# Block 2's accumulators loaded during the projections, and eight of phi_q's last sixteen stores put behind attention's first loads

## The chip, the cores and the metric

The kernel runs on one core of a Trainium2 chip. The metric is the device time of one execution in microseconds. The core has five engines that matter here: TensorE (PE) for matmuls, VectorE (DVE), ScalarE (ACT) and GpSimd (POOL) for elementwise work, and SyncE (SP), whose queue issues nearly all DMA transfers of this kernel. Every engine takes its own instructions strictly in order; an instruction that waits for another engine holds up everything behind it on its own engine.

## The reference

One layer on x of 2048 tokens by 640 features: x is normalised, and the sum of x, a linear attention and an MLP is returned.

```python
def _A_ref(x, wqkv, w_phi, wo):                     # 32 heads of 20
    q, k, v = ...(x @ wqkv)
    pq, pk = q @ w_phi, k @ w_phi                   # per head
    phi_q = concatenate([softmax(pq), softmax(-pq)], -1)
    phi_k = concatenate([softmax(pk), softmax(-pk)], -1)
    kv = einsum("bhsf,bhsd->bhfd", phi_k, v)
    z  = einsum("bhsf->bhf", phi_k)
    o  = (phi_q @ kv) / (phi_q @ z + 1e-6)
    return o @ wo

def _B_ref(x, w1, b1, w2, b2):                      # 640 -> 1728 -> 640
    return gelu(layernorm(x) @ w1 + b1) @ w2 + b2

xn = layernorm(x)
return x + _A_ref(xn, ...) + _B_ref(xn, ...)
```

All values are float32. The kernel splits every float32 operand of a matmul into a high and a low part (`hi`, `lo`) and multiplies high by high, high by low and low by high, three matmuls for each product (`mm3`, lines 69 to 72).

## The kernel before, in words

The 2048 tokens are four blocks of 512, held transposed (features on the 128 partitions). The program has these stages, and the order of work on PE is written out by hand for all of them:

1. The MLP of blocks 0 and 1, with the preparation of the projection weights and of blocks 2 and 3 beside it. At its end the accumulators of both blocks, `acc0` and `acc1`, are stored to DRAM (line 879, the arrays `a0` and `a1`), since their place in SBUF is wanted for something else.
2. The projections (loop at line 1021): for each of 16 token tiles t, four groups i of matmuls (line 910) make q, k and v, already multiplied by the feature map's weights. `k_tile` and `q_tile` make the softmax features with ACT, DVE and POOL; `kv_tile` adds phi_k^T V into five PSUM banks. `q_tile` turns phi_q (DVE, line 1007) into places that lie in the old tiles `acc0` and `acc1` and in one more tile, `et`. Four tiles make one block b; `store_phi(b, n)` (line 1009) writes quarter n of block b to the DRAM array `e`, with four DMAs for each quarter, so sixteen for a block. Block 3's quarters 0 and 1 lie in `acc1`, quarter 2 in `et`, quarter 3 in `acc0`.
3. The first weight pair of the MLP of blocks 2 and 3 (`passes(0, 2)` and `passes(0, 3)`, lines 1106 and 1336). Line 1111 and 1112 load x of these blocks as the accumulators `acc2` and `acc3`, and line 1114 loads combinations of both blocks, `tf`. All of these lie on the right side of SBUF, where the projection weights had been, so their loads wait for the last projection matmul. The coroutine `finish_kv` runs beside the second pass: it issues the sixteen stores of block 3's phi_q, and then turns the kv sums into the attention's weights `kvs` in three groups of small matmuls (lines 1148, 1148 and 1156). Each group has a PSUM bank: the first 3, the second 4, the third 3 again. DVE reads a group's bank with L1138 and L1140 and then helps to split it (ACT L61, DVE L64).
4. Weight pairs 1 to 5 for blocks 2 and 3 together (`Mlp.cross`, lines 420 to 515): seven products of sums of weights and sums of blocks. They go into three banks a, b and c, some of which ACT has to copy out (`copy`, line 455) before the next product may go in. Its weights come from DRAM into the raw tiles r1 and r2 (first layer at line 362, second layer at line 360), are added up into the tile `s` by POOL (`Mlp.sums`, line 393), and are split: ACT makes a high part (line 398), POOL a low part (line 399), but for the sums `s`, where DVE makes it (line 399 too). Attention runs beside these products: `Attention.load` reads phi_q back from `e` (lines 1174 and 1176), `first` splits it (ACT L1205, POOL L1206), and `second` multiplies it by `kvs` on PE (lines 1212 and 1213).
5. The last pair, the output projection and the stores.

Three things set the order around the change. Between lines 877 and 1355 the instructions of DVE, ACT and POOL are put into order by the framework's scheduler, by its own estimate of times; PE's order is the written one throughout, and from line 1355 on that of the other three as well. SP's order is always the scheduler's. Work "beside" PE is attached to ticks: `mlp.tick()` is called after each group of matmuls, and `mlp.after(n, step)` runs a step n ticks later. And `tc.issue_after(x)` keeps what is in it behind the instruction x.

```python
            copy(z22, "b")
            product("a", "s2", "t2")
            copy(z12, "a")
            next(before)
            later[1]()
            next(before)
            product("a", "s3", "t3")
```

These lines (482 to 488) are the part of `cross` where bank a is copied out by ACT and filled again; `later[0]`, called a few lines earlier, is the first half of the split of the pair's second-layer weights.

Of the kernel before, what the change touches and what calls it, by code (L numbers as in the profile page):

```python
# [8 lines left out]
F32 = mybir.dt.float32  # L9
F32R = mybir.dt.float32r  # L10
# [5 lines left out]
P = 128  # L16
S, D, F, H, DH = 2048, 640, 1728, 32, 20
KC = D // P
# [28 lines left out]
def f(ap):  # L47
    return ap.bitcast(F32)
# [3 lines left out]
def tile_kernel(ctx: ExitStack, tc: tile.TileContext, x, xT, wkT, wqT, wv, wphi, wo, w1, b1, w2, b2,  # L52
                ident, mmask, emask, vsel, out):
    nc = tc.nc
# [33 lines left out]
    e_dram = [tc.dram_tile([2 * D, 512], F32, name=f"e{b}") for b in range(NB)]  # L88
# [9 lines left out]
    acc = [None] * NB  # L98
# [18 lines left out]
    rp = ys.enter_context(tc.tile_pool(name="raw", bufs=1))  # L117
# [101 lines left out]
    class Mlp:  # L219
# [166 lines left out]
        def sums(self, g, apart=0):  # L386

            raw = [r.rearrange("p (c f) -> p c f", f=P) for r in self.raw[g, False]]
            (a11, a12), (a21, a22) = ((r[:, 0:4:2, :], r[:, 1:4:2, :]) for r in raw)
            s = rp.tile([P, 3, 2, P], F32, name="s")  # L390
            for i, (out, x0, x1, op) in enumerate(((s[:, 0], a21, a22, ALU.add), (a21, a11, a21, ALU.subtract),
                                                   (s[:, 1], s[:, 0], a11, ALU.subtract), (s[:, 2], a12, s[:, 1], ALU.subtract))):
                self.after(i * apart, lambda out=out, x0=x0, x1=x1, op=op: nc.gpsimd.tensor_tensor(out, x0, x1, op=op))
            self.raw[g, "s"] = s
# [122 lines left out]
    def load_acc(b):  # L517
        nc.sync.dma_start(acc[b], xT[:, b * 512:(b + 1) * 512].rearrange("(c p) t -> p c t", p=P))
# [4 lines left out]
    mlp = Mlp((0, 1, 2, 3), ((0, 2), (1, 3)))  # L523
# [358 lines left out]
    kvp = [banks.tile([P, 512], F32, name=f"bank{i}") for i in (3, 4, 5, 6, 7)]  # L882
    ptile = Banks(0, 1, 2)

    es = ExitStack()
    et = es.enter_context(tc.tile_pool(name="eT", bufs=1, reuse_waits="tile"))
    a = ExitStack()
# [11 lines left out]
    def proj(t, i):  # L899

        yh, yl = y[t // 4]
        c = slice((t % 4) * P, (t % 4) * P + P)
        wh, wl = [w[:, :, slice(*CB[i])] for w in wkv_] if i < 3 else wv_
        ps = ptile()[:, :wh.shape[2]]
        ops = [(lh, rh, kc) for kc in range(KC) for lh, rh in ((yh, wh), (yh, wl), (yl, wh))]
        if i == 3:

            ops.sort(key=lambda op: op[1] is wh)
        for n, (lh, rh, kc) in enumerate(ops):
            nc.tensor.matmul(ps, lh[:, kc, c], rh[:, kc], start=n == 0, stop=n == 3 * KC - 1)  # L910
        return ps
# [97 lines left out]
    def store_phi(b, n):  # L1009

        ed = e_dram[b][320 * n:320 * n + 320, :].rearrange("(j r) (q n) -> q r j n", r=32, q=4)
        for q in range(4):
            nc.sync.dma_start(ed[q], ets[b][n][32 * q:32 * q + 32])  # L1013
# [7 lines left out]
    for t, i in [(t, i) for t in range(14) for i in range(4)] + TAIL:  # L1021
        if (t, i) in ((4, 0), (8, 0)):
            b = t // 4 + 1
            y[b] = [yp.tile([P, KC, 512], F32R, name=f"y{p}{b % 2}") for p in range(2)]
            for p in range(2):
                nc.sync.dma_start(f(y[b][p]), y_dram[b - 2][p])
        ps = proj(t, i)
        pq = 1 + t % 3
        if t and t % 4 == 0:
            store_phi(t // 4 - 1, i)  # L1030
        if i == 0:
            evac = evacuate(ps, 0, 0)
        elif i == 1:
            evac = evacuate(ps[:, :KQ - 512], 0, 512 // H)
            fts[t] = k_tile(t)
            evacuate(ps[:, KQ - 512:], pq, 0)
        elif i == 2:
            evacuate(ps[:, C3 - C2:], pq, B1F)
            v_parts(t, ps, VF)
            q_tile(t)  # L1040
        else:
            evac = v_parts(t, ps, 0)

        tk = {(15, 1): 13, (15, 3): 14}[t, i] if (t, i) in ((15, 1), (15, 3)) else t - 2 if 1 < t < 15 and i == 0 else None
        if tk is not None:
            kv_tile(tk, fts.pop(tk), vbuf[tk % 2])
        if i == 0 and t in (1, 2, 3, 6, 7):

            kc = (1, 2, 3, 6, 7).index(t)
            lo = rp.tile([P, D], F32, name="r1")  # L1050
            hi = rp.tile([P, D], F32R, name="r2")
            nc.sync.dma_start(lo, wo[kc * P:(kc + 1) * P, :])
            with tc.issue_after(evac):
                split(hi, lo.bitcast(F32R), lo, eng=nc.gpsimd)
            for w, wd in zip((f(hi), lo), wo_dram):
                nc.sync.dma_start(wd[:, kc, :], w)
        if (t, i) == (11, 0):
            mlp = Mlp((0, 3, 2, 1), ((1, 2), (0, 3)))
            mlp.ph = ptile
            mlp.fetch_pair(0, False)  # L1060
        if (t, i) == (12, 3):
            with tc.issue_after(evac):
                w1t, parts = mlp.take_pair(0, False, 0)
                for part in parts:
                    part()
            mlp.fetch_pair(0, True)
        if (t, i) == (15, 3):
            w2t, late = mlp.take_pair(0, True, 3)
            late.pop(0)()
# [11 lines left out]

    accp = ctx.enter_context(tc.tile_pool(name="acc23", bufs=1, side="right", reuse_waits="tile"))
    bp = ctx.enter_context(tc.tile_pool(name="bconst", bufs=1, side="right", reuse_waits="tile"))
    for b in range(2, 4):
        acc[b] = accp.tile([P, KC, 512], F32, name=f"acc{b}")
    kvs = bp.tile([P, 11, P], F32R, name="kvs")
    tfp = ctx.enter_context(tc.tile_pool(name="turned", bufs=1, side="right", reuse_waits="tile"))
    tf = [tfp.tile([P, 3, 2, 512], F32R, name=f"tf{q}") for q in range(2)]  # L1090
# [17 lines left out]
        next(before)  # L1108
    for _ in mlp.beside:
        pass  # L1110
    load_acc(2)
    load_acc(3)
    for q in range(2):
        nc.sync.dma_start(f(tf[q]), t_dram[q][:, 1:4])
# [10 lines left out]
    def finish_kv(pxt):  # L1125


        with tc.issue_after(subs["q", 15].ins):
            nc.gpsimd.memset(f(kvs), 0.0)
        for n in range(14):  # L1130
            if n > 9:
                store_phi(3, n - 10)
            yield

        def done(tp, dens, mask, hi, lo):

            r, n, w = tp.shape
            nc.vector.tensor_scalar_add(dens, dens, DEN_EPS)  # L1138
            km = sp.tile([G6, 5, VR], F32, name="km", bufs=1)[:r, :n, :w]
            nc.vector.tensor_tensor(km, tp, mask.unsqueeze(1).to_broadcast(list(km.shape)), op=ALU.mult)  # L1140
            split(hi, lo, km)

        for o in range(2):
            tp = pxt()
            for c in range(5):
                nc.tensor.matmul(tp[:G6, c * VR:(c + 1) * VR], t1[:, c, o], sel, start=True, stop=True)
            kg = kvs[:G6, 0:10].rearrange("p (c o) v -> p o c v", o=2)[:, o]
            done(tp[:G6, :5 * VR].rearrange("p (c v) -> p c v", c=5),  # L1150
                 tp[:G3, :5 * VR].rearrange("p (c a b) -> p c a b", c=5, a=2)[:, :, :, 30:32],
                 mm_t, kg[:, :, 64 * o:64 * o + VR], kg[:, :, 64 - 64 * o:64 - 64 * o + VR])
            yield
        tp = pxt()
        for c, d in ((0, slice(0, 30)), (52, slice(30, 40)), (30, slice(40, 42))):
            nc.tensor.matmul(tp[:80, d], kxs, sel[:XM, c:c + d.stop - d.start], start=True, stop=True)
        tp = tp[:80, :42].unsqueeze(1)
        done(tp, tp[0:40, :, 40:42], em_t, kvs[:80, 10:11, 0:42], kvs[:80, 10:11, 64:106])

    class Attention:  # L1160
# [8 lines left out]
        def load(self, g):  # L1169

            e = self.es[g] = ep.tile([P, 512], F32, name="e", bufs=6)
            r = g * G6
            n = min(P, 2 * D - r)
            nc.sync.dma_start(e[:n], e_dram[self.b][r:r + n, :])
            if n < P:
                nc.sync.dma_start(e[n:], e_dram[self.b][0:P - n, :])

# [152 lines left out]
    at, copies = {}, Banks(3, 4)  # L1330
# [26 lines left out]
    def gathered(g):  # L1357
# [6 lines left out]

        return w2t, [parts[0], second, lambda: g < 5 and mlp.sums(g + 1, 1)]

    for g in range(1, 6):
        w2t, later = gathered(g)
        hid, more = mlp.cross(g, (2, 3), before, later)
        if g < 5:  # L1370
            parts = mlp.splits(g + 1)
        else:
            w1t, parts = mlp.take_pair(6, False, 1)
        for m, _ in enumerate(mlp.second(g, 2, w2t, hid[0])):
            next(more, None)
            if m < len(parts):
                parts[m]()
            if m == 3:
                mlp.fetch_pair(g + 1, True)
        before = mlp.second(g, 3, w2t, hid[1])  # L1380
# [7 lines left out]
    sums, turned, accs = [], {}, {}  # L1388
# [38 lines left out]

    def place_sums():
        sums.append(wp.tile([P, 4, D], F32R, name="w3").rearrange("p i d -> p (i d)"))
        sums.extend([bp.tile([P, 11, P], F32R, name="kvs").rearrange("p i d -> p (i d)"), rp.tile([P, 3, 2, P], F32R, name="s").rearrange("p i k n -> p (i k n)")])  # L1430

    def lo_part(c, k):
        n = (c + 4 * k) * 256
# [233 lines left out]
```

## Time and profile before

| | |
|---|---|
| time, median of 3 runs | 703.58 us (702.67 to 705.65) |
| profiled execution, its own time | 703.39 us |
| its span, first to last instruction | 701.6 us |
| PE busy | 694.9 us (99%) |
| DVE, ACT, POOL busy | 527.6, 365.1, 455.9 us |
| DMA | 107.62 MB, mean 153 GB/s |
| granted TensorE clock, mean | 1.000 |

The page lists busy time, the span in 40 slices, the DMA queues, the chain that ended last, and the costliest groups. In the lists of waits a line names the engine and line that waited and what it waited for. In the timelines each line has the start in us from the span's start, the length in us, engine, source line, operation, output<-input and the count; a bracket at the end says how long the engine was idle before it and what ended that. The span is shorter than the execution's own time by what lies around it.

### The profile page before, as it was taken

Reading aid. Unit: us, or ns where it says so; the run is one execution under the profiler, and the core shown is the slowest. Engines: PE = TensorE matmul, PEld = TensorE weight load, DVE = VectorE, ACT = ScalarE, POOL = GpSimd, SP = SyncE. Lnnn points to the kernel's source line nnn. Section 1 sums busy time; section 2 is a strip of 40 time slices with the busy share of each in tenths; the row PEclk is TensorE's granted clock in tenths of the full one; section 3 lists DMA queues with packets and bytes.
Section 4 is the critical chain, followed back from the end, with each engine's and each line's share of the span. In section 5 each row is a group of like instructions: output and inputs, shape, how many; then the busy total and the mean of one; then the engine's idle time right before and its main releaser. Section 6 shows DMA issues by size and latency. Waiting matters only on the chain.

```text
span 701.6 us, 9805 instructions
## 1 busy us (share of the span) xinstructions
PE 694.9 (99%) x3331; PEld 584.8 (83%) x3331; DVE 527.6 (75%) x859; ACT 365.1 (52%) x617; POOL 455.9 (65%) x388
## 2 busy tenths in 40 slices
PE   9999999999999999999999999999999999999998
PEld 7888888888788888888888888878888888888886
DVE  7868654977744788788888888838688687789783
ACT  6534643344334544554544536557676667659350
POOL 4711314576245997798787969558689997577930
PEclk9999999999999999999999999999999999999999
DMA  9824633485621227425500707974345648881222
GB/s 330 266 100 130 195 105 99 159 276 171 214 105 76 81 89 224 96 80 201 133 1 1 192 0 261 276 226 118 120 146 160 187 145 293 282 283 60 76 76 105
DMA packets 67464, 107.62 MB, mean 153 GB/s; under 512 B 7622, under 2 KB 31974, under 8 KB 65790
## 3 DMA queue, kind: packets, MB, share of 16 engines
q1 hardware_dynamic: 67110, 106.98, 47.6%
q8 instruction: 26, 0.43, 0.2%
q14 instruction: 24, 0.20, 0.1%
q10 hardware_dynamic: 304, 0.01, 0.0%
HBM read 72.42 MB, written 34.55 MB: 152 GB/s over the span
## 4 chain that ended last, share of the span: by engine, by line
PE 75%; DVE 10%; POOL 6%; issue 4%; DMA 3%; ACT 2%; SPq 1%; POOLq 0%; DVEq 0%; ACTq 0%
PE bank L910 17%; PE bank L70 16%; PE bank L72 16%; PE bank L71 16%; POOL m L945 2%; POOL m L956 2%; PE bank L648 2%; PE bank L1212 1%; PE bank L1213 1%; PE bank L980 1%; DVE w L64 1%; SPq L1013 1%; DVE mx L934 1%; DVE acc L1007 1%; PE bank L554 1%
## 5 line engine op out<-in xcount | busy, mean ns | idle before, releaser
L910 PE MATMUL bank<-wkh,y 128*128 128x512 f32 (+1 forms) x480 | 139.5, 364 | 0.0
L70 PE MATMUL bank<-m,w 128*128 128x512 f32 x288 | 113.1, 393 | 0.5 <-DVE acc L337 0.3
L64 POOL TENSOR_TENSOR w<-r,w 128x640 fp32r<-128x640 f32 x32 | 52.6, 1658 | 93.1 <-ACT w L61 62.2
L71 PE MATMUL bank<-m,w 128*128 128x512 f32 x288 | 112.1, 389 | 0.0
L72 PE MATMUL bank<-m,w 128*128 128x512 f32 x266 | 103.6, 389 | 0.0
L70 PE MATMUL bank<-y,w 128*128 128x512 f32 (+1 forms) x256 | 99.6, 389 | 0.0
L71 PE MATMUL bank<-y,w 128*128 128x512 f32 (+1 forms) x256 | 98.9, 386 | 0.0
L910 PEld LDWEIGHTS bank<-wkh,y 128*128 128x128 f32 x480 | 87.5, 188 | 13.3
L72 PE MATMUL bank<-y,w 128*128 128x512 f32 (+1 forms) x246 | 94.9, 386 | 0.0
L910 PE MATMUL bank<-wkl,y 128*128 128x512 f32 (+1 forms) x240 | 87.4, 364 | 0.0
L946 ACT ACTIVATE m<-m,rs_all 128x1280 f32<-128x1280 f32 x32 | 43.7, 1365 | 43.5 <-POOL m L945 43.4
L70 PEld LDWEIGHTS bank<-m,w 128*128 128x128 f32 x288 | 54.1, 188 | 12.5 <-DVE acc L337 0.7
L71 PEld LDWEIGHTS bank<-m,w 128*128 128x128 f32 x288 | 54.1, 188 | 10.9
L72 PEld LDWEIGHTS bank<-m,w 128*128 128x128 f32 x266 | 49.9, 188 | 10.5
L948 DVE TENSOR_REDUCE sm<-m 128x64 f32<-128x1280 f32 x32 | 47.4, 1482 | 14.9 <-ACT m L946 14.8
L910 PE MATMUL bank<-w,y 128*128 128x512 f32 x240 | 57.4, 391 | 0.0
L945 POOL TENSOR_TENSOR m<-m,mx 128x640 f32<-128x640 f32 (+2 forms) x48 | 44.4, 939 | 19.2 <-DVE mx L934 19.2
L70 PEld LDWEIGHTS bank<-y,w 128*128 128x128 f32 x256 | 48.1, 188 | 10.4 <-ACT bank L1280 0.3
L71 PEld LDWEIGHTS bank<-y,w 128*128 128x128 f32 x256 | 48.1, 188 | 9.4
L337 DVE TENSOR_TENSOR acc<-bank,acc 128x512 f32<-128x512 f32 x70 | 46.9, 683 | 11.8 <-PE bank L72 6.6
L72 PEld LDWEIGHTS bank<-y,w 128*128 128x128 f32 x246 | 46.2, 188 | 9.4
L910 PEld LDWEIGHTS bank<-w,y 128*128 128x128 f32 x240 | 44.4, 188 | 8.5
(236 smaller groups left out, 1542.1 us busy)
## 6 DMA issues: line engine op xcount, KB each, us to landing
r<-in_w SPq DMA_DIRECT2D x52, 320.0 KB
e<-e SPq DMA_DIRECT2D x40, 256.0 KB
e<-acc SPq DMA_DIRECT2D x52, 160.0 KB
t<-t SPq DMA_DIRECT2D x8, 512.0 KB
acc<-in_xT SPq DMA_DIRECT2D x3, 1280.0 KB
tf<-t SPq DMA_DIRECT2D x2, 1536.0 KB
xb<-in_x SPq DMA_DIRECT2D x8, 320.0 KB
t<-in_x SPq DMA_DIRECT2D x8, 320.0 KB
```

What stands on the lines that cost most here:

```text
L64: eng.tensor_tensor(lo, src, f(hi), op=ALU.subtract)
L70: nc.tensor.matmul(ps, lh, rh, start=first, stop=False, **kw)
L71: nc.tensor.matmul(ps, lh, rl, start=False, stop=False, **kw)
L72: nc.tensor.matmul(ps, ll, rh, start=False, stop=last, **kw)
L337: nc.vector.tensor_tensor(acc[b][:, m, :], pw, acc[b][:, m, :], op=ALU.add)
L554: nc.tensor.matmul(pz[j], wc[j][wi][:, kc, :], y[0][yi][:, kc, cols], start=(wi, yi, kc) == (0, 0, 0), stop=last[j] == op)
L648: nc.tensor.matmul(ps[:, u * nh * DF:(u + 1) * nh * DF], raw[:nh * DH, u * P:(u + 1) * P], wpt[:nh * DH, g, :nh, 1:], start=True, stop=True)
L910: nc.tensor.matmul(ps, lh[:, kc, c], rh[:, kc], start=n == 0, stop=n == 3 * KC - 1)
L945: subs[n, t] = nc.gpsimd.tensor_tensor(ep[:, s], a, b, op=ALU.subtract)
L946: exps[n, t] = nc.scalar.activation(e, e, AF.Exp, scale=rs_all[:, t:t + 1])
L948: nc.vector.tensor_reduce(sm, e.rearrange("p s (h f) -> p (s h) f", f=DH), axis=AX, op=ALU.add)
L956: nc.gpsimd.tensor_tensor(e3, e3, w.unsqueeze(2).to_broadcast([P, 2 * H, DH]), op=ALU.mult)
```

## The change

Four things are edited. The accumulators of block 2 get a place of their own, allocated ahead of the projections' tiles where the preparation of stage 1 had been, and their load is written inside the projections' loop, at t = 9. Only block 3's stay on the right side. The tile `s` moves from the pool of the raw weights (`rp`) to that of `kvs` (`bp`), which makes up part of the room. In `finish_kv` only quarters 2 and 3 of block 3 are stored; quarters 0 and 1 are stored 12 and 16 ticks into the loop over pairs 1 to 5, behind the last load that attention's block 0 has issued by then.

```diff
@@ -387,7 +387,7 @@
             (a11, a12), (a21, a22) = ((r[:, 0:4:2, :], r[:, 1:4:2, :]) for r in raw)
-            s = rp.tile([P, 3, 2, P], F32, name="s")
+            s = bp.tile([P, 3, 2, P], F32, name="s")
@@ -882,6 +882,7 @@
+    acc[2] = ctx.enter_context(tc.tile_pool(name="acc2", bufs=1)).tile([P, KC, 512], F32, name="acc2")
     es = ExitStack()
@@ -1054,6 +1055,8 @@
+        if (t, i) == (9, 0):
+            load_acc(2)
         if (t, i) == (11, 0):
@@ -1081,10 +1084,9 @@
-    accp = ctx.enter_context(tc.tile_pool(name="acc23", bufs=1, side="right", reuse_waits="tile"))
+    accp = ctx.enter_context(tc.tile_pool(name="acc3", bufs=1, side="right", reuse_waits="tile"))
     bp = ctx.enter_context(tc.tile_pool(name="bconst", bufs=1, side="right", reuse_waits="tile"))
-    for b in range(2, 4):
-        acc[b] = accp.tile([P, KC, 512], F32, name=f"acc{b}")
+    acc[3] = accp.tile([P, KC, 512], F32, name="acc3")
@@ -1108,7 +1110,6 @@
-    load_acc(2)
     load_acc(3)
@@ -1128,7 +1129,7 @@
         for n in range(14):
-            if n > 9:
+            if n > 11:
                 store_phi(3, n - 10)
             yield
@@ -1171,7 +1172,7 @@
-            nc.sync.dma_start(e[:n], e_dram[self.b][r:r + n, :])
+            self.last = nc.sync.dma_start(e[:n], e_dram[self.b][r:r + n, :]).ins
@@ -1364,6 +1365,12 @@
+    def late_store(n):
+        with tc.issue_after(at[0].last):
+            store_phi(3, n)
+
+    for n in range(2):
+        mlp.after(12 + 4 * n, lambda n=n: late_store(n))
     for g in range(1, 6):
@@ -1427,7 +1434,7 @@
-        sums.extend([bp.tile([P, 11, P], F32R, name="kvs").rearrange("p i d -> p (i d)"), rp.tile([P, 3, 2, P], F32R, name="s").rearrange("p i k n -> p (i k n)")])
+        sums.extend([bp.tile([P, 11, P], F32R, name="kvs").rearrange("p i d -> p (i d)"), bp.tile([P, 3, 2, P], F32R, name="s").rearrange("p i k n -> p (i k n)")])
```

No instruction on PE changes its place, and POOL's order stays as well. On three engines the order moves. Lines after 393 are one to three higher in the changed kernel.

SP, from the end of the first pair to the start of `cross`, before (the first of the sixteen stores stands a little ahead, between loads of y; `e_73` is the DRAM array of block 3's phi_q, `e_70` that of block 0; `acc_2046` is `acc1`, `acc_2045` is `acc0`; `r_4360` and `r_4361` are the raw second-layer weights of pair 1, `r_4460` and `r_4461` the first-layer weights of pair 2):

```order
L1013 DMA e_73<-acc_2046 32x10x128 x7
L1013 DMA e_73<-et 32x10x128 x4
L1013 DMA e_73<-acc_2045 32x10x128 x4
L360 DMA r_4360<-in_w 128x640
L360 DMA r_4361<-in_w 128x640
L1174 DMA e<-e_70 80x512
L1176 DMA e<-e_70 48x512
L1174 DMA e<-e_70 128x512 x5
L362 DMA r_4460<-in_w 128x640
L362 DMA r_4461<-in_w 128x640
```

The same place in the changed kernel (`acc_2050` is `acc1` there, `acc_2049` is `acc0`):

```order
L1014 DMA e_73<-et 32x10x128 x4
L1014 DMA e_73<-acc_2049 32x10x128 x4
L360 DMA r_4355<-in_w 128x640
L360 DMA r_4356<-in_w 128x640
L1175 DMA e<-e_70 80x512
L1177 DMA e<-e_70 48x512
L1175 DMA e<-e_70 128x512 x4
L1014 DMA e_73<-acc_2050 32x10x128 x4
L1175 DMA e<-e_70 128x512
L1014 DMA e_73<-acc_2050 32x10x128 x4
L362 DMA r_4459<-in_w 128x640
L362 DMA r_4460<-in_w 128x640
```

Eight stores have moved from ahead of the weights' loads L360 to behind attention's loads, and now stand ahead of the loads L362. Block 2's accumulator load (L518) has moved too: it now stands far ahead, between the two stores of `a0` and `a1` at line 879.

ACT, from the evacuation of block 3's hidden layer (L292, L61) to the kv matmuls, before (`r_4112`, `r_4113` are the raw first-layer weights of pair 1, `s` their sums, `w_4352` and `w_4353` the split weights):

```order
L292 ACTIVATE m_4219<-bank_4221,b1t 128x512
L61 ACTIVATE m_4220<-m_4219 128x512
L292 ACTIVATE m_4219<-bank_4242,b1t 128x512
L61 ACTIVATE m_4241<-m_4219 128x512
L398 ACTIVATE w_4352<-r_4112 128x640
L398 ACTIVATE w_4353<-r_4113 128x640
L61 ACTIVATE kvs<-km 120x5x64
L398 ACTIVATE w_4353<-s 128x768
```

The same place in the changed kernel:

```order
L292 ACTIVATE m_4222<-bank_4224,b1t 128x512
L398 ACTIVATE w_4347<-r_4117 128x640
L61 ACTIVATE m_4223<-m_4222 128x512
L292 ACTIVATE m_4222<-bank_4245,b1t 128x512
L61 ACTIVATE m_4244<-m_4222 128x512
L398 ACTIVATE w_4348<-r_4118 128x640
L398 ACTIVATE w_4348<-s 128x768
L61 ACTIVATE kvs<-km 120x5x64 x2
```

The first split of pair 1's weights has moved up by three places, and the split of the sums stands ahead of both splits of `kvs`.

DVE at the kv matmuls, before (`bank_4301` is the bank of the first group, `bank_4315` of the second, `bank_4331` of the third; L335 adds a finished bank to block 2's accumulators):

```order
L335 SCALAR_TENSOR_TENSOR acc_4123<-bank_4281,b2t,acc_4123 128x512
L1138 TENSOR_SCALAR bank_4301<-bank_4301 60x10x2
L1140 TENSOR_TENSOR km<-bank_4301,mm_t 120x320
L335 SCALAR_TENSOR_TENSOR acc_4123<-bank_4297,b2t,acc_4123 128x512
L1138 TENSOR_SCALAR bank_4315<-bank_4315 60x10x2
L64 TENSOR_TENSOR kvs<-km,kvs 120x5x64
L1140 TENSOR_TENSOR km<-bank_4315,mm_t 120x320
L1138 TENSOR_SCALAR bank_4331<-bank_4331 40x2
L399 TENSOR_TENSOR w_4353<-s,w_4353 128x768
```

The same place in the changed kernel:

```order
L335 SCALAR_TENSOR_TENSOR acc_2026<-bank_4276,b2t,acc_2026 128x512
L399 TENSOR_TENSOR w_4348<-s,w_4348 128x768
L1139 TENSOR_SCALAR bank_4296<-bank_4296 60x10x2
L1141 TENSOR_TENSOR km<-bank_4296,mm_t 120x320
L335 SCALAR_TENSOR_TENSOR acc_2026<-bank_4292,b2t,acc_2026 128x512
L64 TENSOR_TENSOR kvs<-km,kvs 120x5x64
L1139 TENSOR_SCALAR bank_4310<-bank_4310 60x10x2
L1141 TENSOR_TENSOR km<-bank_4310,mm_t 120x320
```

The low part of the sums, L399, has moved from behind all three groups to ahead of the first group's evacuation.

## Rows read from the trace of the kernel before

**Rows 1.** The page's part 1: busy us (share of the span) xinstructions.

```profile
PE 694.9 (99%) x3331; PEld 584.8 (83%) x3331; DVE 527.6 (75%) x859; ACT 365.1 (52%) x617; POOL 455.9 (65%) x388
```

**Rows 2.** The waits of PE: engine, line, waited for: us, times, longest us.

```profile
PE bank L582 <- POOL m L580: 1.3, 1, 1.3
PE bank L70 <- ACT m L455: 1.2, 1, 1.2
PE bank L70 <- DVE acc L337: 0.3, 1, 0.3
```

**Rows 3.** PE in order of time, 463.8 to 466.1: start, length, instruction [idle before].

```profile
463.83 0.39 PE L71 MATMUL bank<-m,w 128*128 128x512 f32 x1
464.06 0.39 PE L72 MATMUL bank<-m,w 128*128 128x512 f32 x1
465.67 0.50 PE L70 MATMUL bank<-tf,w 128*128 128x512 f32 x1 [1.22 <-ACT m L455]
```

**Rows 4.** ACT in order of time, 459 to 466.

```profile
459.24 0.63 ACT L464 ACTIVATE m<-m 128x512 fp32r<-128x512 f32 x1
462.28 0.74 ACT L398 ACTIVATE w<-r 128x640 fp32r<-128x640 f32 x1 [2.41 <-DMA r<-in_w]
462.93 0.58 ACT L455 ACTIVATE m<-bank 128x512 f32<-128x512 f32 x1
464.50 0.63 ACT L1205 ACTIVATE m<-e 128x512 fp32r<-128x512 f32 x1 [1.00 <-DMA e<-e]
465.04 0.58 ACT L455 ACTIVATE m<-bank 128x512 f32<-128x512 f32 x1
```

**Rows 5.** SP's queue in order of time, 446 to 469: issues of DMAs.

```profile
446.66 4.91 SPq L1013 DMA_DIRECT2D e<-acc  x7
...
454.58 2.93 SPq L1013 DMA_DIRECT2D e<-acc  x4
457.63 1.31 SPq L360 DMA_DIRECT2D r<-in_w  x2
...
460.01 2.59 SPq L1174 DMA_DIRECT2D e<-e  x5
464.69 3.69 SPq L362 DMA_DIRECT2D r<-in_w  x2
```

**Rows 6.** POOL in order of time, 444 to 475.

```profile
444.32 0.74 POOL L393 TENSOR_TENSOR s<-r 128x256 f32<-128x256 f32 x1 [1.67 <-DMA r<-in_w]
447.87 1.81 POOL L399 TENSOR_TENSOR w<-r,w 128x640 fp32r<-128x640 f32 x1 [2.81 <-ACT w L398]
...
451.83 1.83 POOL L399 TENSOR_TENSOR w<-r,w 128x640 fp32r<-128x640 f32 x1
...
474.29 0.75 POOL L393 TENSOR_TENSOR s<-r 128x256 f32<-128x256 f32 x1
```

**Rows 7.** Stretch by stretch: busy us (x) of PE, PEld, DVE, ACT, POOL; PEclk, DMA share, GB/s.

```profile
200.00:220.00 20.00, 20.00 (x94) 16.85 (x93) 9.08 (x18) 5.86 (x11) 10.58 (x11) 1.00 0.32 132
```

**Rows 8.** ACT in order of time, 444 to 453.

```profile
444.30 0.69 ACT L292 ACTIVATE m<-bank,b1t 128x512 f32<-128x512 f32 x1 [2.34 <-DVE m L64]
445.08 0.63 ACT L61 ACTIVATE m<-m 128x512 fp32r<-128x512 f32 x1
...
447.06 0.73 ACT L398 ACTIVATE w<-r 128x640 fp32r<-128x640 f32 x1
...
451.91 0.85 ACT L398 ACTIVATE w<-s 128x768 fp32r<-128x768 f32 x1 [0.41 <-POOL s L393]
```

**Rows 9.** DVE in order of time, 449 to 455.

```profile
449.26 0.18 DVE L1138 TENSOR_SCALAR bank<-bank 60x20 f32<-60x20 f32 x1 [0.33 <-PE bank L1148]
449.48 0.49 DVE L1140 TENSOR_TENSOR km<-bank,mm_t 120x320 f32<-120x320 f32 x1
...
452.80 1.68 DVE L399 TENSOR_TENSOR w<-s,w 128x768 fp32r<-128x768 f32 x1
```

**Rows 10.** PE in order of time, 449 to 452: the third kv group.

```profile
451.57 0.53 PE L1156 MATMUL bank<-sel,kxs 123*80 123x30 f32 x6
```

## The prediction

> **What bounds the kernel now.** The engine part of the page comes first: PE is busy for 694.9 of the 701.6 us of the span [rows 1]. The other four engines have room, so only what makes PE stand still, or what puts work onto it, can move the time. The change adds and removes no matmul; what it can win is therefore in the waits of PE [rows 2]. Two of them are longer than half a microsecond: 1.3 us right at the start of the program, before the warming matmuls, which nothing in the change touches, and 1.2 us "PE bank L70 <- ACT m L455". The next one is 0.3 us. So the ceiling of any gain is one stall.
>
> Where that stall lies is read from PE in order of time [rows 3]: the matmul at 464.06 is followed by the next only at 465.67, where the one before it had come 0.23 us earlier, at 463.83. The stall costs 465.67 - 464.06 - 0.23 = 1.38 us. It is the place in `cross` of pair 1 where the third product goes into a bank that ACT has to copy out first (L455).
>
> ACT tells why the copy is late [rows 4]. ACT takes its work in order. After L464 at 459.24 the next instruction is L398, the first half of the split of pair 1's second-layer weights, and it starts at 462.28 after 2.41 us of idle time for "DMA r<-in_w". Only behind it stand the copy of the second bank (462.93), a split of attention's first group (464.50, another 1.00 us for a DMA) and, at 465.04, the copy that PE waits for. So ACT stood for 3.4 us in all for two DMAs whose instructions only happen to be ahead of that copy.
>
> Why the weights are late stands in SP's queue [rows 5]: the loads L360 are issued at 457.63, right behind the sixteen stores of phi_q's last block, which go out 0.70 us apart (seven in 4.91). The load landed at 462.28, 4.65 us after its issue.
>
> **The change part by part.** *Half of the stores goes behind.* Eight of sixteen stores now stand ahead of L360. If the first goes out at 446.66 as it did, L360 follows at 446.66 + 8 x 0.70 = 452.3, and its data is there at 452.3 + 4.65 = 456.9. ACT asks for it at 459.24 + 0.63 = 459.9. The raw tiles that it overwrites must be free: the last reader of the second is the POOL split at 451.83, which ended at 453.66 [rows 6] and comes earlier in the changed kernel, as shown below. At worst L360's second load goes at 453.7, which is still in time. Both DMA waits of ACT go, and with them the 1.38 us. Cover: some 3 us.
>
> *Block 2's accumulators come early.* This load of 1280 KB moves to the start of the projections, between the two stores of blocks 0 and 1. The DMA engines are busy for 0.32 of that stretch [rows 7] and no matmul there needs it; block 1's store, behind it on SP, waits for an add of its own anyway. I cost it at nothing. At the end of the projections the same bytes no longer stand ahead of pair 1's first-layer weights. POOL waited 1.67 us for those, until 444.32 [rows 6]; that wait goes, but POOL then waited 2.81 us for ACT's L398 before its next instruction at 447.87, so by itself it would give nothing.
>
> *The scheduler answers to that.* Between the projections and attention it orders ACT and DVE by its own estimate, and it now expects these weights sooner. On ACT the first L398 is moved ahead of two evacuations of block 3. It started at 447.06, behind L61 at 445.08 [rows 8]; now it can start once L292 (444.30) lets it, between 444.95 (two independent instructions start some 0.65 apart, as at 462.28 and 462.93 [rows 4]) and 445.08. It is 2.0 to 2.1 us earlier, and so is the chain that hangs on it: POOL's split at 447.87, the sums, ACT's split of them at 451.91, and POOL's last split at 451.83.
>
> On DVE the low part of the sums, L399, is moved from behind the three groups of kv matmuls to ahead of the first one's evacuation. It started at 452.80, just after ACT's L398 of 451.91 had ended [rows 8, 9]; 2.1 us earlier is 450.7. But DVE reaches it before 449.26, where it evacuated the first group before (L1138, L1140). DVE takes its work in order, so L1138 and L1140, ready at 449.26, now stand behind an instruction that waits until 450.7.
>
> Who waits for that: the third group, L1156, writes into the bank of the first, which L1140 has to have read. L1156 began at 451.57 [rows 10], without a wait. Now: L399 lasted 1.68 us, because POOL's split (451.83, ending 453.66) ran beside it; DVE ended at 454.48, 0.82 after POOL did. With both 2.1 us earlier, POOL ends at 451.6 and DVE at 452.4; L1138 and L1140 take 0.22 and 0.49, and L1156 starts at about 453.0. PE stands for 1.4 us. The lower bound is L399 alone, 0.82 from 450.7, so 451.5, 452.2 for L1140 and a stall of 0.7; the upper one is the smaller shift (2.0), so 1.5, and a first matmul behind the stall as long as the one at 465.67 (0.50 instead of 0.39 [rows 3]), 1.6. I take 1.4, since both instructions move together and the row shows the pair.
>
> The Trainium skill speaks of this pair, in "SBUF — State Buffer", section "SBUF: two separate sides": a DVE instruction with two SBUF inputs and a GpSimd instruction that reads SBUF exclude each other, and the later one waits for the whole of the earlier. The trace agrees: DVE ends 0.82 after POOL [rows 6, 9]. By that rule the stall is 1.4; if the two shared, it would be nearer to 0.7.
>
> *The late stores and the place of s.* The other eight stores come behind the first loads of attention. One load of attention stands among them, of its fifth group. On SP there was room between 460.01 + 2.59 = 462.6 and the next load at 464.69 [rows 5], and the 5.4 us by which everything ahead is earlier come to that. The tile s moves to another pool, and its instructions stay; 0.
>
> **Sum.** Against the profiled execution (703.39 us, of which the span is 701.6): -1.38 for the old stall, +1.4 for the new one, 0 for the rest: 703.4 us. From the bounds of the new stall, 0.7 to 1.6, it is 702.7 to 703.6. That execution stands 0.2 below the median of the runs, 703.58. PE's later work even starts at the same time as before: what was 1.4 late at 453 absorbs the slot where PE stood at 464.
>
> **The rivals.** *The new stall does not form* (0.16). If the sums were ready by about 449 on DVE, or the bank were free otherwise, only the gain is left: 703.39 - 1.38 = 702.0. For it speaks that the scheduler chose this order; against it, that ACT could not start L398 before 444.30 because it waited 2.34 us there for DVE [rows 8], which the change leaves.
>
> *Both stalls* (0.05). If the weights of L360 slipped by more than the 3 us of cover, the old wait would stand beside the new: 703.39 + 1.4 = 704.8. Against it: eight stores fewer.
>
> *The late stores hold up the next weights* (0.05). This is the way to a slower kernel. SP takes its queue in order too: the eight stores (5.6 us) stand between attention's loads and L362, the first-layer weights of pair 2. POOL adds them at 474.29 [rows 6]. L362's second load was issued by 464.69 + 3.69 = 468.4 and, with 4.65 us to land, was there at 473.0; the slack is 1.3 us. If the stores pushed it back by all of their 5.6 us, POOL would stand for 4.3 us, the splits of attention behind it too, and PE would wait for those: 707.7. From 1.3 us of delay on it decides. Against it: SP was idle for 2.1 us ahead of L362, attention's loads now start earlier, and the second load of L362 was issued only at the end of a row of 3.69 us, which is a wait for the tile that it overwrites and not the queue.
>
> That the change does not do what it says is hardly a case: the order of SP shows the load and the stores moved.
>
> **How the numbers follow.** The forecast has 0.74, the rivals 0.16, 0.05 and 0.05. A measurement of this kernel can tell about 0.5%, 3.5 us, from no change. Only the last rival is beyond it, so slower has 0.05; faster by 3.5 us would need more waits than PE has (0.02, for what no row shows); the same has 0.93. The range takes in the forecast's bounds, the first two rivals and the spread of the medians: 701.8 to 705.0.
>
> **What would show it.** Right: the wait of PE for ACT's L455 in pair 1's `cross` is gone; ACT's L398 there starts without a DMA wait; a new wait of PE of 0.7 to 1.6 us at L1156's line (now L1157) for DVE's L1140 (now L1141), with L399 before that on DVE, idle ahead of it for ACT; L360 issued near 452. Wrong: no wait at that line (702.0), a wait of POOL for L362's data near 474, or a wait for DMA on ACT near 460.

## The result, and the profile after

| | before | changed |
|---|---|---|
| median | 703.37 us of 22 runs | 705.44 us of 22 runs |
| lowest, highest | 702.50, 705.65 us | 703.61, 709.00 us |
| ratio of the times | | 1.0026, 95% interval 1.0018 to 1.0035 |
| profiled execution | 703.39 us | 704.24 us |
| its span | 701.6 us | 702.5 us |

The changed kernel is slower by 0.26%. That is inside the half per cent of the forecast, but outside its range: 705.0 was the end, and 703.4 the number. Its runs fall into two groups. Of the 22, 16 have a mean granted TensorE clock of 0.998 or less, and they lie at 705.1 us and above; the six others, at 0.999 to 1.000, lie between 703.6 and 704.4. The profiled execution is one of the six. So there are two differences to explain: 0.85 us (704.24 - 703.39) that this profile can show, and the 1.2 us from there to the median, which it cannot. Of the 0.85 us, 0.44 stand at DVE's last add (698.77 against 698.33); the rest lies behind it, where only the last stores of the output are under way.

Up to line 882 both kernels have the same line numbers; L1138, L1140, L1156 and L1212 of the kernel before are L1139, L1141, L1157 and L1213 here. The waits of PE in the changed kernel, columns as in [rows 2]:

```profile
PE bank L1157 <- DVE km L1141: 2.1, 1, 2.1
PE bank L582 <- POOL m L580: 1.3, 1, 1.3
PE bank L186 <- DVE xb L172: 0.4, 1, 0.4
```

The wait for ACT's L455 is gone from the list. In its place stands the wait at L1157 that the prediction described, but it is longer than it said. PE in order of time there, with [rows 10] as the counterpart:

```profile
450.90 0.40 PE L72 MATMUL bank<-m,w 128*128 128x512 f32 x1
453.44 0.56 PE L1157 MATMUL bank<-sel,kxs 123*80 123x30 f32 x6 [2.14 <-DVE km L1141]
```

The next matmul would have come 0.23 us after the first: the stall is 453.44 - 450.90 - 0.23 = 2.31 us. DVE shows why, in order of time; [rows 9] are its counterpart:

```profile
446.47 1.46 DVE L64 TENSOR_TENSOR m<-m,m 128x512 fp32r<-128x512 f32 x1
...
448.51 1.25 DVE L64 TENSOR_TENSOR m<-m,m 128x512 fp32r<-128x512 f32 x1
449.68 0.74 DVE L335 SCALAR_TENSOR_TENSOR acc<-bank,b2t,acc 128x512 f32<-128x512 f32 x1
451.26 1.42 DVE L399 TENSOR_TENSOR w<-s,w 128x768 fp32r<-128x768 f32 x1 [0.84 <-ACT w L398]
452.60 0.17 DVE L1139 TENSOR_SCALAR bank<-bank 60x20 f32<-60x20 f32 x1
452.80 0.49 DVE L1141 TENSOR_TENSOR km<-bank,mm_t 120x320 f32<-120x320 f32 x1
```

L399 stands idle for ACT's split of the sums, L1139 and L1141 stand behind it, and the bank comes free only with L1141. ACT, the counterpart of [rows 8]:

```profile
444.41 0.69 ACT L292 ACTIVATE m<-bank,b1t 128x512 f32<-128x512 f32 x1 [2.85 <-PE bank L72]
445.00 0.73 ACT L398 ACTIVATE w<-r 128x640 fp32r<-128x640 f32 x1
...
450.38 0.85 ACT L398 ACTIVATE w<-s 128x768 fp32r<-128x768 f32 x1 [1.09 <-POOL s L393]
```

And POOL, which stands between these two, the counterpart of [rows 6]:

```profile
445.80 1.57 POOL L399 TENSOR_TENSOR w<-r,w 128x640 fp32r<-128x640 f32 x1 [2.19 <-ACT w L398]
447.34 1.17 POOL L393 TENSOR_TENSOR r<-r,r 128x256 f32<-128x256 f32 x1
448.47 0.74 POOL L393 TENSOR_TENSOR s<-s,r 128x256 f32<-128x256 f32 x1
449.29 1.06 POOL L393 TENSOR_TENSOR s<-r,s 128x256 f32<-128x256 f32 x1
450.30 1.56 POOL L399 TENSOR_TENSOR w<-r,w 128x640 fp32r<-128x640 f32 x1
```

ACT's first L398 is 2.06 us earlier than before (445.00 against 447.06), and POOL's first split 2.07 us (445.80 against 447.87). But ACT's split of the sums is only 1.53 us earlier (450.38 against 451.91): between the two POOL lost half a microsecond. In the kernel before, this chain began only during the second of DVE's two L64, which took 0.65 and 0.68 us there, and POOL's adds took 0.72 to 0.74 us (the first and the third are shown):

```profile
446.36 0.65 DVE L64 TENSOR_TENSOR m<-m,m 128x512 fp32r<-128x512 f32 x1
...
447.58 0.68 DVE L64 TENSOR_TENSOR m<-m,m 128x512 fp32r<-128x512 f32 x1
```

```profile
449.64 0.73 POOL L393 TENSOR_TENSOR r<-r,r 128x256 f32<-128x256 f32 x1
...
451.14 0.74 POOL L393 TENSOR_TENSOR s<-r,s 128x256 f32<-128x256 f32 x1
```

Now both L64 run against POOL's split and adds, and the two engines take turns. POOL's L399 ends at 445.80 + 1.57 = 447.37, DVE's first L64 at 447.93 and POOL's first L393 at 448.51; POOL's second L393 ends at 449.21, DVE's second L64 at 449.76 and POOL's third L393 at 450.35. Within each of these two rows of three, each ends 0.55 to 0.6 us after the one of the other engine, whatever its start.

On the other side, the old stall has gone the way that was forecast. SP and ACT in the changed kernel, counterparts of [rows 5] and [rows 4]:

```profile
451.55 1.40 SPq L360 DMA_DIRECT2D r<-in_w  x2
```

```profile
461.14 0.63 ACT L464 ACTIVATE m<-m 128x512 fp32r<-128x512 f32 x1
461.68 0.73 ACT L398 ACTIVATE w<-r 128x640 fp32r<-128x640 f32 x1
462.31 0.60 ACT L455 ACTIVATE m<-bank 128x512 f32<-128x512 f32 x1
```

L360 is issued 6 us earlier, and ACT's L398 follows L464 without a wait for a DMA.

### The profile page after: what moved, and what is told of

Its sections match the earlier page's. It is cut to its first block, busy times and chain, and to the rows that moved or that the text cites. A ratio compares the mean times of both kernels' runs of the same rounds, so it can differ in the third digit from the quotient of the medians.

```text
span 702.5 us, 9802 instructions
## 1 busy us (share of the span) xinstructions
PE 694.3 (99%) x3331; PEld 584.5 (83%) x3331; DVE 527.2 (75%) x859; ACT 366.1 (52%) x617; POOL 457.0 (65%) x388
## 4 chain that ended last, share of the span: by engine, by line
PE 95%; DVE 2%; issue 1%; POOL 1%; DMA 0%; ACT 0%; POOLq 0%; DVEq 0%
PE bank L911 28%; PE bank L70 19%; PE bank L71 18%; PE bank L72 18%; PE bank L981 3%; PE bank L648 2%; PE bank L1213 1%; PE bank L1214 1%; PE bank L554 1%; PE bank L313 1%; PE bank L333 1%; PE bank L332 1%; PE bank L314 1%; DVE st L138 0%; DMA xb<-in_x 0%
## 5 line engine op out<-in xcount | busy, mean ns | idle before, releaser
L64 POOL TENSOR_TENSOR w<-r,w 128x640 fp32r<-128x640 f32 x32 | 52.7, 1660 | 93.4 <-ACT w L61 62.5
L72 PE MATMUL bank<-m,w 128*128 128x512 f32 x266 | 103.6, 389 | 0.0
L72 PE MATMUL bank<-y,w 128*128 128x512 f32 (+1 forms) x246 | 95.0, 386 | 0.0
L72 PEld LDWEIGHTS bank<-m,w 128*128 128x128 f32 x266 | 49.9, 188 | 10.5
L72 PEld LDWEIGHTS bank<-y,w 128*128 128x128 f32 x246 | 46.2, 188 | 9.4
L1207 POOL TENSOR_TENSOR e<-e,m 128x512 fp32r<-128x512 f32 x28 | 41.8, 1496 | 15.2 <-ACT m L1206 15.2
```

What stands on the lines that cost most here:

```text
L64: eng.tensor_tensor(lo, src, f(hi), op=ALU.subtract)
L72: nc.tensor.matmul(ps, ll, rh, start=False, stop=last, **kw)
L1207: mlp.after(1, lambda: nc.gpsimd.tensor_tensor(pl, e, f(ph), op=ALU.subtract))
```

## The experiments

The theory: what costs is that PE stands at L1157 behind L399 on DVE, and that in most executions PE's clock falls to the lower level after that standstill. The rivals: the late stores beside attention's first loads cost the time; the early load does; the lower clock has nothing to do with the standstill.

**The changed kernel once more** (no edit).

> The changed kernel once more, beside the three variants. Its 22 runs so far lie in two groups: 703.6 to 704.4 us at a granted clock of 0.999 to 1.000, and 705.1 to 706.3 at 0.997 to 0.998. Theory: the 2.3 us that TensorE stands at L1157 gives about +0.9 net of the old stall, and in most executions the granted clock falls after that gap, which gives the rest. Expected 705.4 median (703.8 to 706.3 single runs); if the profiled execution is one of the 0.997 ones, a stretch at the 1.2 GHz level just behind 453 us. Rival (the lower clock has nothing to do with the gap): the stretch at the lower level lies elsewhere, or is spread.

Measured: 705.57 us (703.50 to 706.50, 12 runs), ratio 1.0025, interval 1.0014 to 1.0036. Eight of 12 runs have a clock of 0.997 or 0.998 (median 705.7), four have 0.999 or 1.000 (median 703.9). With the 22 runs above that is 24 of 34 at the lower clock. The profiled execution was again one at 0.999, so that it doesn't show where the clock falls; that question stays open for this kernel itself. It shows PE at L72 at 452.12 and at L1157 at 454.12: a stall of 1.77 us.

**L399 held back.** All of the change is kept, and DVE's low part of the sums is put behind the third kv group's evacuation, its place before.

```diff
-        def split(self, hi, lo, src, eng=nc.gpsimd):
+        def split(self, hi, lo, src, eng=nc.gpsimd, behind=None):
...
-            self.after(1, lambda: eng.tensor_tensor(lo, src, f(hi), op=ALU.subtract))
+            def low():
+                with ExitStack() as st:
+                    if behind is not None:
+                        st.enter_context(tc.issue_after(behind))
+                    eng.tensor_tensor(lo, src, f(hi), op=ALU.subtract)
+            self.after(1, low)
...
-            nc.vector.tensor_scalar_add(dens, dens, DEN_EPS)
+            evacs.append(nc.vector.tensor_scalar_add(dens, dens, DEN_EPS).ins)
...
-    for part in mlp.splits(1):
+    for part in mlp.splits(1, evacs[2]):
```

> Both parts of the change kept, only VectorE's low part of pair 1's sums (L399, here L404) put behind the third kv group's L1139 (here L1148), where it stood in the kernel before. Theory (the loss is the wait at L1157 and what the clock does after it): no wait of over 0.5 us there, none at L455 either; 702.0 us (701.7 to 702.5), granted clock as in the kernel before, single runs in one group. Rival A (late stores beside attention's loads are the cost): stays at 704 or above. Rival B (the early load of the accumulators, or the second group of runs, has its cause elsewhere): 702 in some runs and 703.5 in most, clock 0.997 as in the changed kernel.

Measured: 702.00 us (701.72 to 702.64, 12 runs), ratio to the kernel before 0.9975, interval 0.9966 to 0.9985; all 12 runs at 0.999 or 1.000. PE goes through the place without a wait, as the timeline shows (L1166 is the third group here):

```profile
451.17 0.40 PE L72 MATMUL bank<-m,w 128*128 128x512 f32 x1
451.41 0.53 PE L1166 MATMUL bank<-sel,kxs 123*80 123x30 f32 x6
451.79 0.48 PE L70 MATMUL bank<-m,w 128*128 128x512 f32 x1
```

One instruction's place on DVE makes the difference between 705.5 and 702.0 us, and with it goes every run at the lower clock. Neither the late stores nor the early load can be the cost by themselves, since both are in this kernel.

**The early load and the place of `s` alone.** The sixteen stores are where they were before.

```diff
-            if n > 11:
+            if n > 9:
...
-    for n in range(2):
-        mlp.after(12 + 4 * n, lambda n=n: late_store(n))
```

> The accumulators' early load and the place of s alone; all 16 stores of phi_q where the kernel before has them. VectorE's order is that of the changed kernel. Theory: the wait at L1157 is there with about 2.3 us; TensorE then comes to pair 1's first products after the late high part that it waited for in the kernel before (464.06 - 0.43 + 2.31 = 465.94 against 465.67), so that the old wait is covered by the new one: 704.0 to 704.4 at a clock of 1.000, and a median near 705.4 with the same two groups. Rival A (the late stores are the cost): 703.4 or less. Rival C (the two waits add up): 705.7 at full clock.

Measured: 704.67 us (703.86 to 707.56, 12 runs), ratio 1.0021, interval 1.0009 to 1.0033. Six runs at 0.999 or 1.000 have a median of 704.1, six at 0.995 to 0.997 one of 705.9. The median near 705.4 that was expected is missed: half of the runs and not two thirds are at the lower clock, so the median falls between the groups. The groups themselves lie where those of the changed kernel lie. The profile has no wait for L455. It is one at the lower clock, in which PE comes to that place later still; for the runs at the full clock their time speaks, 704.1 and not the 705.7 that two waits in a row would give. So the wait and the lower clock come with this part of the change alone. And this time the profiled execution (705.81 us, mean clock 0.997) is one at the lower clock. PE in order of time:

```profile
451.31 0.40 PE L72 MATMUL bank<-m,w 128*128 128x512 f32 x1
453.39 0.56 PE L1157 MATMUL bank<-sel,kxs 123*80 123x30 f32 x6 [1.69 <-DVE km L1141]
...
454.37 0.54 PE L72 MATMUL bank<-m,w 128*128 128x512 f32 x1
454.70 0.63 PE L70 MATMUL bank<-m,w 128*128 128x512 f32 x1
455.13 0.63 PE L71 MATMUL bank<-m,w 128*128 128x512 f32 x1
...
457.69 0.48 PE L71 MATMUL bank<-y,w 128*128 128x512 f32 x1
458.01 0.39 PE L72 MATMUL bank<-y,w 128*128 128x512 f32 x1
458.23 0.39 PE L70 MATMUL bank<-y,w 128*128 128x512 f32 x1
```

and the same stretch by microseconds (columns as in [rows 7]; the number after POOL's is the granted clock):

```profile
452.00:453.00 1.00, 0.00 (x0) 0.00 (x0) 0.97 (x3) 0.00 (x0) 0.00 (x0) 1.00 0.95 260
453.00:454.00 1.00, 0.60 (x7) 0.64 (x8) 1.00 (x3) 0.47 (x1) 0.00 (x0) 1.00 0.96 255
454.00:455.00 1.00, 1.00 (x4) 0.81 (x4) 0.95 (x4) 0.05 (x1) 0.00 (x0) 0.73 0.98 208
455.00:456.00 1.00, 1.00 (x4) 0.72 (x4) 0.54 (x2) 0.42 (x1) 0.00 (x0) 0.50 0.97 246
456.00:457.00 1.00, 1.00 (x4) 0.81 (x3) 0.71 (x2) 0.24 (x1) 0.00 (x0) 0.50 0.66 167
457.00:458.00 1.00, 1.00 (x4) 0.79 (x3) 0.49 (x1) 0.00 (x0) 0.00 (x0) 0.56 0.83 157
458.00:459.00 1.00, 1.00 (x6) 0.82 (x5) 0.36 (x2) 0.00 (x0) 0.70 (x1) 1.00 1.01 262
```

PE stands from 451.54 to 453.39 and resumes, and about a microsecond later the granted clock is 0.5, the 1.2 GHz level. The matmuls then come 0.43 us apart instead of 0.23. From 454.37 to 458.01 nine steps take 3.64 us; at 0.227 they would take 2.04. That is 1.6 us, which no list of waits shows, since PE counts as busy there.

**The late stores alone.** The kernel before with these lines, and neither the load nor the tile moved:

```diff
-            if n > 9:
+            if n > 11:
...
+    def late_store(n):
+        with tc.issue_after(at[0].last):
+            store_phi(3, n)
+
+    for n in range(2):
+        mlp.after(12 + 4 * n, lambda n=n: late_store(n))
```

> The kernel before with the late stores alone; accumulators and s as before, and VectorE's order as before. Theory: pair 1's weights are issued some 5 us earlier, the wait of 1.6 us at L455 goes, and no wait at L1157 takes its place: 702.0 us (701.7 to 702.5), clock as in the kernel before. Rival A (late stores beside attention's first loads are the cost): 704 to 705.5. Rival D (the earlier weights alone do not end the old wait, since the sums on GpSimd stand in its way): 703.4.

Measured: 701.68 us (701.17 to 702.82, 12 runs), ratio 0.9974, interval 0.9965 to 0.9982; all at 0.999 or 1.000. Here PE runs through both places:

```profile
451.10 0.40 PE L72 MATMUL bank<-m,w 128*128 128x512 f32 x1
451.33 0.53 PE L1156 MATMUL bank<-sel,kxs 123*80 123x30 f32 x6
...
463.82 0.39 PE L72 MATMUL bank<-m,w 128*128 128x512 f32 x1
464.05 0.39 PE L70 MATMUL bank<-tf,w 128*128 128x512 f32 x1
```

The second pair is the place of [rows 3], where PE stood before. All of the gain is in the late stores, and this kernel has the lowest median of the study.

**The third group in another bank.** L399 stands ahead of the first group's evacuation, as in the changed kernel. Only the wait for bank 3 is taken away. This kernel and the ones after it were timed on another chip than the four above; the kernel before has 703.32 us there against 703.38, with 4 of 35 runs at 0.998 or less against 2 of 35, and the changed kernel itself was not timed there with them.

```diff
-        tp = pxt()
+        tp = banks.tile([P, 512], F32, name="bank1")
         for c, d in ((0, slice(0, 30)), (52, slice(30, 40)), (30, slice(40, 42))):
```

> The changed kernel with the third kv group written into bank 1 instead of bank 3; the order of every engine is that of the changed kernel, so VectorE still has L399 ahead of the first group's evacuation. Theory (what costs is that the third group waits for bank 3 behind L399): no wait of over 0.5 us at L1157, 701.9 to 702.2 us, one group of runs with a clock of 0.999 to 1.000, as with L399 held back (702.0). Rival (L399's early place costs by itself, through what stands behind it on VectorE): a wait of 0.7 to 2 us at a later bank, L70 behind L335 or L455, and 703 or more.

Measured: 702.19 us (701.67 to 702.77, 12 runs), ratio 0.9978, interval 0.9968 to 0.9987; all at 0.999 or 1.000. There is no wait at L1157 (L72 at 451.83, L1157 at 452.07), though DVE's L1141 still comes late, at 453.21. So L399's early place by itself costs nothing that these runs show (702.19 us against 702.00 with L399 held back); the bank that PE needs back does.

**PE kept at work while it waits.** In the changed kernel, nine products of the identity with itself, or four, go into bank 1 ahead of the third group; nobody reads them.

```diff
+        fill = banks.tile([P, 512], F32, name="bank1")
+        for n in range(9):
+            nc.tensor.matmul(fill[:, :P], idt, idt, start=True, stop=True)
         tp = pxt()
```

> The changed kernel with nine products of the identity with itself (128x128, float32) into bank 1 just ahead of L1157, read by nobody: the third group still waits for bank 3, but TensorE works through most of the 2.3 us. Theory (the lower clock follows TensorE's standing still): nearly all runs at a clock of 0.999 to 1.000, 703.6 to 704.3 us, median 703.9; idle time at L1157 below 0.5 us. Rival (the lower clock comes from the work that runs in the stretch, or is chance): two thirds of the runs at 0.997 to 0.998 and a median of 705.4 as before. If the fill is longer than the wait, up to 0.3 more.

Measured with nine: 704.01 us (703.72 to 704.52), all 12 runs at 0.999 or 1.000, ratio 1.0006, interval 0.9996 to 1.0016.

```profile
451.65 2.17 PE L1157 MATMUL bank<-idt 128*128 128x128 f32 x18
453.66 0.55 PE L1160 MATMUL bank<-sel,kxs 123*80 123x30 f32 x6
```

> The same with four products instead of nine: TensorE stands for about 1.2 to 1.4 us, about what the kernel before has at L455 (1.38). Theory: the runs at 0.997 become as rare as with the kernel before (2 of 35 there against 24 of 34 here), median 703.9 to 704.2. Rival (any gap at this place brings the lower clock): half of the runs or more at 0.997 and a median above 705.

Measured with four: 704.10 us (703.58 to 705.23), again all 12 at 0.999 or 1.000, ratio 1.0008, interval 0.9997 to 1.0018. The run of 705.23 has a clock of 1.000, so not every late run is one at the lower clock.

```profile
451.35 1.05 PE L1157 MATMUL bank<-idt 128*128 128x128 f32 x8
453.54 0.56 PE L1160 MATMUL bank<-sel,kxs 123*80 123x30 f32 x6 [1.14 <-DVE km L1141]
```

The third group is delayed by 2.0 and 2.2 us, as in the changed kernel (2.3 and 1.8), and the useless products shorten nothing. The median is 1.5 us lower all the same, and no run is at the lower clock. This shows that the second part of the loss comes with PE standing still, and not from the work around it, as far as the two chips can be compared. The share of runs at 0.998 or less in all kernels, against the longest standstill in this region:

| kernel | PE stands | runs at 0.998 or less |
|---|---|---|
| stores alone, L399 held back, other bank | none | 0 of 36 |
| nine products | none | 0 of 12 |
| four products | 1.1 us | 0 of 12 |
| before (in the two comparisons of these experiments) | 1.4 us at L455 | 6 of 70 |
| `s` alone | 1.3 us at L455 | 1 of 12 |
| load and `s` alone | 1.9 us at L1157 | 6 of 12 |
| changed kernel | 1.8 and 2.3 us at L1157 | 24 of 34 |

The first 22 runs of the kernel before have no clock on record; four of them lie at 705.5 to 705.7 us, apart from the other 18, which end at 704.2. And no profile shows an execution of the kernel before at the lower clock, so that its clock falls behind L455 is not shown.

**The place of `s` alone.** The kernel before, with the tile taken from `bp`.

```diff
-            s = rp.tile([P, 3, 2, P], F32, name="s")
+            s = bp.tile([P, 3, 2, P], F32, name="s")
...
```

> The kernel before with the tile s in the other pool alone: accumulators and all stores as before. It moves L398 up on ScalarE by two places and L399 on VectorE up to the place behind the first kv group's evacuation, not ahead of it. Theory (the wait needs L399 ahead of L1140): no wait at L1156, the old wait at L455 with 1.2 us, 703.2 to 703.7 us, clock as in the kernel before. Rival (an earlier L399 is enough, by the second group or its evacuation): a new wait of 0.7 us or more near 452 and, with the old one covered by it, 703.5 to 705.

Measured: 703.57 us (702.98 to 705.80, 12 runs), ratio 0.9993, interval 0.9978 to 1.0007. DVE takes L399 behind the first group's L1140 here, and PE has only the old wait:

```profile
463.49 0.39 PE L72 MATMUL bank<-m,w 128*128 128x512 f32 x1
464.98 0.50 PE L70 MATMUL bank<-tf,w 128*128 128x512 f32 x1 [1.11 <-ACT m L455]
```

So an earlier L399 is not enough; it has to stand ahead of the instruction that frees bank 3. With the place of `s` alone the scheduler doesn't put it there, with the early load beside it it does. Whether the early load alone would bring it to that is not shown: the load with `s` left in its old pool was not tried.

## Why the prediction was wrong

**What bounds the kernel** was read rightly as far as the engine goes: the time follows PE in the eight runs. But beside PE's waits its clock counts, as shown below.

**The old stall, -1.38,** was right in place, cause and size. With the new stall taken away, the change gives 702.00 and 702.19 us against 703.38 and 703.32: -1.4 and -1.1. With the late stores alone it is -1.7. The profiles tell it more closely. In the kernel before, PE in order of time:

```profile
451.33 0.40 PE L72 MATMUL bank<-m,w 128*128 128x512 f32 x1
...
469.88 0.39 PE L1212 MATMUL bank<-m,kvs 128*128 128x512 f32 x1
```

The first is the matmul ahead of the third kv group, the second attention's first product; between their starts lie 18.55 us. In the three kernels that have neither stall it is 17.03, 17.03 (L399 held back, stores alone) and 17.04 us (other bank), so the old stall was worth 1.5 us in each, and what their medians differ by lies outside this stretch. The rival "the new stall does not form" had 702.0 for this case.

**The early load, 0,** was right as far as the profiles show. The DMA share between 200 and 220 us went from 0.32 [rows 7] to 0.57, and PE stays busy for the whole of it:

```profile
200.00:220.00 20.00, 20.00 (x95) 16.93 (x94) 9.34 (x17) 5.84 (x11) 11.03 (x11) 1.00 0.57 198
```

From there to the third kv group PE neither gains nor loses: the same matmul starts at 205.15 us against 205.59 before, and another at 448.60 against 449.04, both 0.44 us earlier.

**The late stores, 0 beside their gain,** were right as well; POOL takes pair 2's weights at 474.68 us without a wait for a DMA, and the rival of 707.7 did not come.

**The new stall, +1.4 (0.7 to 1.6),** is the term that failed first. Its mechanism was right row by row, and its size was not. By the medians at the full clock the third group's wait costs 703.9 to 704.1 (changed kernel and the two with products) less 702.0 to 702.2 (held back, other bank), so about 1.9 us; the profiles of the changed kernel and of load and `s` alone have waits of 1.8, 1.9 and 2.3. The stretch of 17.03 us takes 18.86 and 19.36 us in the changed kernel, 19.07 and 19.28 us with the products, 1.8 to 2.3 more. The step that went wrong is "and so is the chain that hangs on it". It took the chain to move as one piece by 2.0 to 2.1 us. The head did (2.06), but the chain was moved into a stretch where DVE had its two L64, and POOL and DVE slowed each other: 0.65 became 1.46 us, and 0.73 (POOL's L393 at 449.64 before) became 1.17. ACT's split of the sums came 1.53 us earlier instead of 2.1, and L399 started at 451.26 instead of 450.7. A smaller slip is in the sum itself: DVE's end at 452.4 with 0.22 and 0.49 behind it gives 453.1 and a stall of 1.5, a tenth more than was taken. The Trainium skill, "SBUF — State Buffer", section "SBUF: two separate sides", states the exclusion that the prediction used for L399 at the end of this chain. The rows agree here too: DVE's L64, which starts while POOL's L399 runs, ends 0.56 us after it, and takes 1.46 us in place of 0.65. The prediction did not ask it of the chain's new neighbours. That this is what makes the difference of 0.5 us is read from the rows, and was not tried by a run of its own. In the profile of 2.31 us PE also came to the place 0.44 us earlier than before (451.13 against 451.57), which lengthens the wait there, but not the delay.

**A term that the sum did not have at all** is the clock. The prediction valued a stall of PE at its length. In the one profile that shows it, of the load and `s` alone, a stall of 1.85 us had a stretch at the 1.2 GHz level behind it, which cost 1.6 us. In the changed kernel 24 of 34 executions have the lower mean clock; that their stretch lies at the same place is inferred from the variants without the standstill, which have none, and no profile shows it. With 1.6 us for it the sum is 703.4 - 1.4 + 1.9 + 1.6 = 705.5, against medians of 705.44 and 705.57, which lie in the larger of the two groups. The two stalls that were set against each other as equal, 1.38 and 1.4, were not of one kind: with the old one the mean clock mostly stayed up (all but 6 of 70 executions), with the new one it mostly fell. At one place, L1157, the standstill of 1.1 us (four products) has no run at the lower clock and that of 1.8 to 2.3 us has most of them, which speaks for the length; that the old and the new stall also stand at different places in the program was not separated further.

## What to carry to other kernels

Price a standstill of the busiest engine by what it does to the clock too: here two stalls that differ by half a microsecond differed by two in the time of most executions, and the wait lists show only the first part. When a chain is moved earlier, look at what the other engines do in its new place before shifting all its rows by one number. And when a change has two parts, time each alone: here the late stores alone are worth 1.7 us, and the early load with `s`, through one instruction's place on DVE, takes 3.5 us away beside them (705.5 against 702.0).

## What was not expected of the hardware

Work that nobody needs went with a faster kernel: with nine products of 128x128, placed in a wait that they don't shorten, the median was 704.01 us against 705.57 without them, and the granted clock stayed at its upper level in all 12 runs. And one program, the changed kernel, falls into two groups of times 1.5 to 1.9 us apart, which the mean granted clock (0.999 or more against 0.998 or less) tells apart run by run.
